# First folds by 128 columns, and the last left rows stored from GpSimd's queue

## Chip, cores, metric

One core of one Trainium2 chip. The metric is device time in microseconds of a whole launch; lower is better. Names in the profile: PE is the matmul engine (TensorE), DVE is VectorE, ACT is ScalarE; SyncE (SP) only issues DMAs (transfers between memories) and waits for them here.

## The reference, cut to what matters

```python
# four batches of N = 5824 rows, C = 256 channels
qn, kn = q / norm(q, axis=1), k / norm(k, axis=1)
a   = softmax(kn.T @ qn)                 # 256 x 256 per batch
x   = (v @ a).reshape(23296, 256)
out = ((x @ w1) * (x @ w2)) @ w3 @ w_out # d_ff = 1024
```

The kernel never forms `v @ a`. It *folds* the softmax matrix into the weights, `Wf = a @ [w1 | w2]` (256 x 2048 per batch), and multiplies v by that. Likewise `w3 @ w_out` is one matrix W. N is 45 x 128 + 64, so each batch ends in 64 "left" rows; the left rows of two batches are handled together.

## The kernel before, where the change and the argument touch it

Nearly all loads of q, k, v and the weights are issued by GpSimd; they cast f32 to bf16 on the way. An *eviction* below is the copy that takes a matmul's result out of its accumulation buffer. In batch 0 the softmax comes as soon as q and k are in, and the first folds stand between it and the first product tile:

```python
def quarter_mm(lo, c1, c2):                  # 256 columns of w1 and of w2
    ...
    for w in range(2):
        nc.tensor.matmul(m[:, w, :], lhsT=e[:, c2, c1 block], rhs=w12[:, c2, w, lo:lo+256], ...)
    if c2 == CT - 1:                         # evicted in two pieces of 128 columns
        for o in (0, P) if lo == 0 else ...:
            if c1 == 0: nc.scalar.activation(out=dst, in_=src, func=AF.Copy, scale=rs[:, c1])
            else:       nc.vector.tensor_scalar_mul(dst, src, rs[:, c1])

def first_folds():
    sum_mm(0)                                # row sums over the first half of the channels
    for c1 in range(CT): quarter_mm(0, c1, 0)
    sum_mm(1)                                # second half, then rs = 1 / sums
    for c1 in range(CT): quarter_mm(0, c1, 1)
```

The end of the kernel (`emit_out`, the small last chunk of a pair of batches; `B - 1` is the last batch):

```python
nc.vector.tensor_copy(o2, tl[1][:, 0, :])            # left rows of both batches
for m in (b - 1, b):
    k = (m - b + 1) * LEFT
    nc.sync.dma_start(out=out[m*N + NT*P : (m+1)*N, :], in_=o2[k : k + LEFT, :])
...
nc.scalar.copy(o[:, 0, :], tl[0][:, 0, :])
other = nc.scalar if b == B - 1 else nc.sync
other.dma_start(out=rows[:, NT - 1, :], in_=o[:, 0, :])
```

After this the framework adds, on each engine, a drain and a handshake that GpSimd collects. The drain is an instruction at the end of the engine's work: DVE's, for example, runs from 563.50 to 563.96 us, until just after DVE's last copy, which ends at 563.91.

## Time and profile before

| | before |
|---|---|
| time, median of 5 runs | 569.44 us (569.25 to 569.69) |
| span of the profiled execution | 567.7 us |
| PE busy | 557.6 us, 98% of the span, at a granted clock of 0.999 |
| chain that ended last | PE 93%, DMA 5%, ACT 1% |
| GpSimd's DMA instructions | 97, the last one at 492.32 us |

The prediction below takes the span apart, with the lines of the profile on which it rests.

### The profile page before, as it was taken

How to read it: one execution, taken by the hardware profiler on the slowest of the kernel's cores; microseconds unless marked ns; L12 is line 12 of the kernel's file. 1: busy time of each engine (PE TensorE's matmuls, PEld its weight loads, DVE VectorE, ACT ScalarE, POOL GpSimd, SP SyncE). 2: the span in 40 equal slices, each digit the busy share in tenths (PEclk: the TensorE clock that was granted, in tenths of full speed). 3: DMA queues.
4: the chain of work that ended last, by engine and by line, in shares of the span. 5: the costliest groups of instructions: out<-in, count | busy, mean ns of one | idle time of the engine just before them, and what ended most of it. 6: DMA issues, size and time to landing. Idle time of an engine off the chain costs nothing.

```text
span 567.7 us, 10095 instructions
## 1 busy us (share of the span) xinstructions
PE 557.6 (98%) x3755; PEld 355.4 (63%) x3755; DVE 375.4 (66%) x581; ACT 338.7 (60%) x627; POOL 77.9 (14%) x163
## 2 busy tenths in 40 slices
PE   8799999999999999999999999999999999999997
PEld 5664566776656666666656566666655655665655
DVE  1047645888966577888766668787876665565564
ACT  1057536777766577777675567777765554454453
POOL 4260013120111111121210101030120000000000
PEclk9999999999999999999999999999999999999999
DMA  9999989978455796595661595765740325221011
GB/s 213 211 182 209 173 171 237 226 164 192 115 142 121 143 192 148 90 193 123 145 149 75 97 219 117 155 120 121 185 112 39 85 74 149 64 68 71 38 70 61
DMA packets 75104, 77.45 MB, mean 136 GB/s; under 512 B 54192, under 2 KB 58800, under 8 KB 75056
## 3 DMA queue, kind: packets, MB, share of 16 engines
q0 software_dynamic: 15760, 38.93, 39.3%
q1 hardware_dynamic: 59008, 37.23, 22.0%
q10 hardware_dynamic: 288, 0.66, 0.4%
q8 instruction: 29, 0.48, 0.3%
q14 instruction: 19, 0.16, 0.1%
HBM read 78.91 MB, written 23.86 MB: 181 GB/s over the span
## 4 chain that ended last, share of the span: by engine, by line
PE 93%; DMA 5%; ACT 1%; POOL 0%; issue 0%; DVE 0%; ACTq 0%; POOLq 0%
PE o L521 28%; PE b L476 28%; PE a L476 28%; PE G L192 5%; DMA k<-in_k_dram 5%; PE fold L363 2%; PE w L649 1%; ACT kr L283 0%; PE quarter L389 0%; POOL k L111 0%; POOL q L111 0%; PE sqk L225 0%; PE row L271 0%; ACT e L322 0%; ACT Wf L398 0%
## 5 line engine op out<-in xcount | busy, mean ns | idle before, releaser
L497 DVE TENSOR_TENSOR abs<-as,b 128x512 bf16<-128x512 bf16 x336 | 230.6, 687 | 143.9 <-ACT as L482 131.4
L482 ACT CAST as<-a 128x512 bf16<-128x512 f32 (+1 forms) x384 | 215.9, 562 | 170.4 <-DVE abs L497 84.7
L476 PEld LDWEIGHTS <-Wf 128*128 128x128 bf16 x1536 | 149.0, 98 | 102.3 <-ACT Wf L398 0.6
L476 PE MATMUL a<-vT,Wf 128*128 128x512 bf16 x704 | 209.6, 379 | 0.4 <-ACT Wf L398 0.4
L476 PE MATMUL b<-vT,Wf 128*128 128x512 bf16 x704 | 209.6, 379 | 0.0
L521 PE MATMUL o<-W_sb,abs 128*128 128x256 bf16 x1344 | 201.5, 273 | 0.0
L521 PEld LDWEIGHTS <-abs 128*128 128x128 bf16 x1344 | 131.2, 98 | 79.8 <-issue 0.2
L201 DVE TENSOR_TENSOR acc<-acc,sq 128x1024 f32<-128x1024 f32 x66 | 80.4, 1219 | 0.6 <-ACT sq L189 0.6
L192 PE MATMUL G<-k,q 128*128 128x256 bf16 x276 | 49.8, 273 | 0.0
L189 ACT ACTIVATE sq<-q 128x512 f32<-128x512 bf16 x66 | 41.8, 633 | 0.0
L189 ACT ACTIVATE sq<-k 128x512 f32<-128x512 bf16 x66 | 41.5, 629 | 0.0
L464 POOL COPY gate_t<-abs 1x1 bf16<-1x1 bf16 x39 | 10.5, 269 | 171.7 <-DVE abs L497 168.8
L543 DVE COPY osb<-o 128x512 f32<-128x512 f32 x44 | 30.1, 685 | 0.9 <-PE o L521 0.9
L192 PEld LDWEIGHTS <-q 128*128 128x128 bf16 x276 | 27.0, 98 | 3.1
L542 ACT COPY osb<-o 128x512 f32<-128x512 f32 x44 | 25.8, 586 | 4.1 <-PE o L521 2.1
L468 POOL COPY gate_t<-vT 1x1 bf16<-1x1 bf16 x16 | 3.1, 193 | 158.8 <-DMA vT<-v 158.8
L111 POOL DMA_DIRECT2D q<-in_q_dram x28 | 15.1, 540 | 12.5 <-DMA k<-in_k_dram 5.5
L370 ACT ACTIVATE Wf<-fold,rs 128x512 bf16<-128x512 f32 x15 | 10.3, 687 | 10.9 <-PE fold L363 8.7
L283 ACT ACTIVATE kr<-row 128x256 f32<-128x256 f32 x1 | 0.4, 383 | 26.1 <-PE row L271 26.1
L363 PE MATMUL fold<-w,e 128*128 128x512 bf16 x56 | 15.0, 379 | 0.0
L487 DVE TENSOR_TENSOR left<-as,b 128x192 bf16<-128x192 bf16 x32 | 11.3, 354 | 5.1 <-ACT as L482 2.7
L497 DVE TENSOR_TENSOR abq<-as,b 128x512 bf16<-128x512 bf16 x16 | 10.8, 686 | 5.0 <-ACT as L482 4.5
(98 smaller groups left out, 242.3 us busy)
## 6 DMA issues: line engine op xcount, KB each, us to landing
out_dram<-osb SPq DMA_DIRECT2D x44, 512.0 KB, 3.3
k<-in_k_dram POOLq DMA_DIRECT2D x19, 512.0 KB, 8.3
v<-in_v_dram POOLq DMA_DIRECT2D x19, 512.0 KB, 5.2
q<-in_q_dram POOLq DMA_DIRECT2D x18, 512.0 KB, 5.8
w_wout<-in_moe_w_dram POOLq DMA_DIRECT2D x1, 2048.0 KB, 22.7
k<-in_k_dram POOLq DMA_DIRECT2D x4, 320.0 KB, 8.8
v<-in_v_dram POOLq DMA_DIRECT2D x4, 320.0 KB, 4.9
q<-in_q_dram POOLq DMA_DIRECT2D x3, 320.0 KB, 4.1
```

Of the source, the lines that this page charges most:

```text
L111: nc.gpsimd.dma_start(out=pieces[nm, n, pi][:, lo:hi, :], in_=qk_main[nm, n][0][:, pi * PIECE + lo : pi * PIECE + hi, :])
L189: nc.scalar.activation(out=dst[:, :, part, :], in_=src[:, o : o + 2, :], func=AF.Square)
L192: nc.tensor.matmul(G[:, ct, :], lhsT=qt[:, i, ct * P : (ct + 1) * P], rhs=kt[:, i, :], start=(pr == 0 and part == 0 and ct == 0), stop=(pr ...
L201: nc.vector.tensor_add(accs[n], accs[n], sqs[0])
L363: nc.tensor.matmul(m, lhsT=st["e"][:, c2, c1 * P : (c1 + 1) * P], rhs=w12[:, c2, w, lo:hi], start=(c2 == 0), stop=(c2 == CT - 1),)
L476: nc.tensor.matmul(t[:, :n], lhsT=Wf[b][:, ct, w, j * P : (j + 1) * P], rhs=rhs_of(b, c, ct), start=(ct == 0), stop=(ct == CT - 1),)
L482: nc.scalar.copy(a_sb[:, :n], tiles[0][:, :n])
L487: nc.vector.tensor_mul(both, a_sb[:, :n], tiles[1][:, :n])
L497: nc.vector.tensor_mul(ab, a_sb, tiles[1])
L521: nc.tensor.matmul(tl[h][:, o, :], lhsT=lhsT, rhs=W_sb[:, j, :], start=(j == 0 and o == 0), stop=(j == FT - 1 and (small or o == 1)), skip ...
L542: nc.scalar.copy(o[:, 0:2, :], tl[0])
L543: nc.vector.tensor_copy(o[:, 2:4, :], tl[1])
```

## The change

The intent: fold only the 128 columns that the first product tile needs, so that it starts sooner; and let the last two left stores leave side by side on two queues instead of one after the other on SyncE's.

```diff
-        def quarter_mm(lo, c1, c2):
+        def columns_mm(lo, width, c1, c2):
...
-                    m[:, w, :], lhsT=..., rhs=w12[:, c2, w, lo : lo + 256],
+                    m[:, w, :], lhsT=..., rhs=w12[:, c2, w, lo : lo + width],
...
         def first_folds():
             sum_mm(0)
             for c1 in range(CT):
-                quarter_mm(0, c1, 0)
+                columns_mm(0, P, c1, 0)
             sum_mm(1)
             for c1 in range(CT):
-                quarter_mm(0, c1, 1)
+                columns_mm(0, P, c1, 1)
+            for c1 in range(CT):
+                for c2 in range(CT):
+                    columns_mm(P, P, c1, c2)
...
-                        nc.sync.dma_start(out=out[m * N + NT * P : (m + 1) * N, :], in_=o2[k : k + LEFT, :])
+                        eng = nc.gpsimd if m == B - 1 else nc.sync
+                        eng.dma_start(out=out[m * N + NT * P : (m + 1) * N, :], in_=o2[k : k + LEFT, :])
```

More of the change, by code (lines that the diff above doesn't have):

```diff
@@ L378, in fold @@
                 fold_mm((w, c1, h * 512, (h + 1) * 512), c2, tag, i % 2 == 0 or (n == 0 and i == 7))
-        def quarter_mm(lo, c1, c2):
+        def columns_mm(lo, width, c1, c2):
             if c2 == 0:
-                tag = "ab" if lo == 0 else "out"
+                tag = "ab" if lo < 256 else "out"
                 st[lo, c1] = psum.tile(
-                    [P, 2, 256], F32, tag=tag, name=f"quarter_{lo}_{c1}", bufs={"ab": 4, "out": 3}[tag]
+                    [P, 2, width], F32, tag=tag, name=f"columns_{lo}_{c1}", bufs={"ab": 4, "out": 3}[tag]
                 )
@@ L389, in quarter_mm @@
                 nc.tensor.matmul(
-                    m[:, w, :], lhsT=st["e"][:, c2, c1 * P : (c1 + 1) * P], rhs=w12[:, c2, w, lo : lo + 256],
+                    m[:, w, :], lhsT=st["e"][:, c2, c1 * P : (c1 + 1) * P], rhs=w12[:, c2, w, lo : lo + width],
                     start=(c2 == 0 and w == 0), stop=(c2 == CT - 1 and w == 1), skip_group_check=True,
@@ L393, in quarter_mm @@
             if c2 == CT - 1:
-                for o in (0, P) if lo == 0 else (slice(0, 256),):
-                    cols = slice(o, o + P) if lo == 0 else o
-                    dst, src = Wf[n][:, c1, :, lo : lo + 256][:, :, cols], m[:, :, cols]
-                    if c1 == 0:
-                        nc.scalar.activation(out=dst, in_=src, func=AF.Copy, scale=st["rs"][:, c1 : c1 + 1])
-                    else:
-                        nc.vector.tensor_scalar_mul(dst, src, st["rs"][:, c1 : c1 + 1])
+                dst = Wf[n][:, c1, :, lo : lo + width]
+                if c1 == 0:
+                    nc.scalar.activation(out=dst, in_=m, func=AF.Copy, scale=st["rs"][:, c1 : c1 + 1])
+                else:
+                    nc.vector.tensor_scalar_mul(dst, m, st["rs"][:, c1 : c1 + 1])
         def first_folds():
@@ L412, in second_quarter @@
                 for c2 in range(CT):
-                    quarter_mm(256, c1, c2)
+                    columns_mm(256, 256, c1, c2)
         if n == 0:
```

## The prediction

> **What bounds the kernel now.** I read the page first: PE is busy 98% of a 567.7 us span at a granted clock of 0.999, and the chain that ended last is PE for 93% and DMA for 5%. The next question is where PE is *not* the bound. A table of stretches answers it:
>
> ```profile
> 30.45:37.27 6.82, 6.04 (x64) 4.56 (x64) 3.08 (x12) 3.46 (x10) 6.54 (x10) 1.00 1.17 157
> ...
> 563.66:567.68 4.02, 0.00 (x1) 0.00 (x0) 0.25 (x1) 0.37 (x1) 0.00 (x0) 0.81 0.24 65
> ```
>
> The columns are stretch and length, then busy time of PE, weight loads, DVE, ACT and POOL. The stretch between these two, 37.27 to 563.66, asked for by itself, has PE busy 526.36 of 526.39 us. So whatever moves the first product matmul at 37.27 moves all that follows, and only three pieces are not PE's: the input loads to 30.45 (untouched), the softmax and first folds to 37.27, and the tail of 4.02 us after the last matmul. The change touches the second and the third.
>
> The chain of waits in the second piece, in order of time (start, length, what):
>
> ```profile
> 35.18 0.52 ACT e L322
> 35.70 0.05 issue
> 35.75 0.20 PE sum L340 x2
> 35.95 0.46 PE quarter L389 x4
> 36.41 0.04 PE sum L340 x2
> 36.45 0.02 issue
> 36.47 0.18 DVE rs L348
> 36.65 0.02 issue
> 36.68 0.02 ACTq L398
> 36.69 0.04 issue
> 36.74 0.48 ACT Wf L398
> 37.22 0.05 issue
> 37.27 0.60 PE a L476 x2
> ```
>
> What to see: the four 256-column matmuls of the first half of the sum over channels (0.46 us) stand between the first and the second pair of row-sum matmuls; the row sums give the reciprocal, the reciprocal gives the eviction, and that gives the first product. Evictions are already 128 columns wide per w; the matmuls are not.
>
> The third piece, from the timeline and from the instructions of the kernel's end:
>
> ```profile
> 563.48 0.42 DVE L533 COPY oleft<-o 128x256 f32<-128x256 f32 x1 [0.55 <-PE o L521]
> ...
> 563.93 1.13 SPq L536 DMA_DIRECT2D out_dram<-oleft  x2
> 564.10 0.36 ACTq L540 DMA_DIRECT2D out_dram<-osb  x1
> ```
>
> ```profile
> L765 POOLq DRAIN x3: 46/102/8672, 492.2 to 567.4; - x3
> L765 SPq DRAIN x3: 7/7/13, 566.8 to 567.2; - x3
> L765 PEldq DRAIN x2: 13/369/725, 563.0 to 567.2; - x2
> ```
>
> SyncE issues the two left-row stores one after the other (starts 563.93 and 564.48). Its own waits in the trace pass at 566.25 (first left store, 2.31 after its start), 566.58 (ACT's 128 KB, 2.48 after 564.10) and 566.75 (second left store, 2.27). A closing handshake follows to 567.68; GpSimd collects it, and from its wait at 566.94 to the end are 0.74 us. The measured time is the span plus about 1.76 us (569.45 for the profiled execution).
>
> The second fence is the surprise. Its columns are count, min/median/max in ns, first and last start. Each engine ends with a drain. GpSimd's first one took **8672 ns**, and the order of records makes that one the start at 492.20, behind its last DMA instructions (491.80 and 492.32, the latter done generating at 492.88). It ended at 500.87, which is 8.0 us after the last descriptors and 4.4 us after that transfer landed (SyncE's wait for it passes at 496.43). GpSimd's other drains, with no DMA before them, took 102 and 46 ns. Today all this lies under 66 us of matmuls.
>
> **What the Trainium skill says.** (1) "TensorE: Matmul & The Clock Gate", section "Back-to-back issue gap": 134 cycles at 128 columns, 262 at 256, thus 56 and 109 ns at 2.4 GHz, though it gives 81 ns per matmul for a sustained stream with weight loads. The trace agrees with the first: the 128-column transposes start 55 ns apart, the 256-column folds 108. (2) "DMA: Bandwidth & Descriptors", section "Issuing engines are not separate DMA queues": queues share the same 16 engines and a second issuer saves only sequencer time. Here that is the 0.55 us between SyncE's two starts. (3) The same page, "Anatomy of one DMA — SWDGE (gpsimd) path": about 2.0 us fixed, mostly the receipt of the write. The 32 KB load that GpSimd issued at 491.80 landed in 1.9. (4) "VectorE: DVE Perf Modes", section "The DRAIN you can't avoid", says the drains at a kernel's ends are about 12 ns on all engines. SyncE's 7 and 13 ns agree; GpSimd's 8672 does not, and the measurement decides. No page that I found tells what that drain waits for.
>
> **Part one: the folds.** Nothing is removed in columns: eight 256-column matmuls become sixteen of 128. At 55 ns that is 16 x 0.055 = 0.88 us against 8 x 0.108 = 0.87. Evictions keep size and number (four of 473/466 ns on ACT and 484/474 on DVE). What moves:
> - The first four now take 4 x 0.055 = 0.22 and end their issue at about 36.03. The second exp ends at 36.09 and its weight load starts 0.05 later, at 36.14, already set by ACT. Only the row-sum matmul, now at 36.24, was held up by the fold in front, so it moves to about 36.15: **0.09 us**, not the 0.22 that the shorter folds suggest.
> - Reciprocal, ACT's semaphore and eviction follow: eviction 36.74 to about 36.65. Its own matmul ends issue near 36.27 plus 0.22 of latency = 36.49, no new bound. DVE's eviction of the other half, today 36.93 because its 256-column matmul ends late, moves to about 36.65 too; it needs 0.48 and ends at 37.13, beside ACT's.
> - The first product goes from 37.27 to about 37.18. The added second block of eight, 0.44 us from about 36.43, ends by 36.90, inside the hole in which PE waits for the eviction, so it costs nothing.
> - Buffers: the ring of four now has the four column tiles ahead of the first two product tiles. Those reuse exactly the tiles whose evictions they need anyhow.
> - Carried to the end? The nearest operand is the load that the transposes at 44.50 need: it lands at 34.76 + 9.6 = 44.36, 0.14 ahead, enough for 0.09.
>
> Part one: **-0.09 us**.
>
> **Part two: the store.** Removed from SyncE: one issue of 0.58 us. Added to GpSimd: one of about 0.53 us, after the same DVE copy (ends 563.91, or 563.82 shifted). From a GpSimd copy's end at 491.46 to the end of the following descriptors at 492.33 were 0.86 us, and the first packet came 0.70 later; elsewhere the first figure is as low as 0.67. So descriptors end near 564.6, packets start near 565.3 and, with the 1.16 us that SyncE's first left store took from first packet to landing, it lands near 566.4. ACT's store, unchanged at 566.58 - 0.09 = 566.49, would then land last. The gain is at most 566.75 - 566.58 = 0.17 us, not the 0.55 of the issue.
>
> Against it stands the drain, which now must follow this last store. If it takes 8.0 us after the last descriptors again: 564.6 + 8.0 = 572.6, + 0.74 = 573.3 span, + 1.76 = 575.1. If it takes 4.4 after landing instead: 566.4 + 4.4 = 570.8, + 0.74 + 1.76 = 573.3. I take the drain as real work that repeats, since it stands behind DMA instructions alone.
>
> **The rivals.**
> - *No drain of that length.* It may hang on the larger transfers before it (320 KB) or on something else that ended near 500.9 (SyncE's 0.52 us store issue ends then). For: one occurrence only, and a record of a sequencer instruction. Against: the two short drains had no DMA. Then 569.44 - 0.09 - (0 to 0.17) = 569.2 to 569.35. Chance 0.28.
> - *GpSimd's queue is slow to begin but the drain short*: a landing after 566.8 would give 569.4 to 569.8. The 1.9 us of the small load speaks against it. Within the same 0.28.
> - *The drain scales with outstanding bytes*: 64 KB instead of 352 KB would give something between, 570 to 573. Chance about 0.15. What is left, 0.57, is the two readings worked out above.
> - *Narrow matmuls at 81 ns* instead of 55: 16 x 0.081 = 1.3 us; the second block would end at 36.15 + 12 x 0.081 = 37.12, still inside the hole. The loss is nil, the gain stays.
>
> **Range and chances.** A small heap at about 569.3 (0.28), a thin stretch to 573 (0.15) and a large heap from 573 to 575.2 (0.57, the 8.0 reading more likely than the 4.4). The mixture has half its weight on each side at about 573.5 to 574; I give 574.0, which stands between the two drain readings. A range that holds 8 in 10 has to reach both heaps: 569.0 to 575.5. Two per cent are 11.4 us. The gains come to under 0.3 us and the worst drain reading costs 575.1 - 569.4 = 5.7, so "same" is nearly sure.
>
> **What would show it.** First product at 37.15 to 37.20, the second exp's row sum at about 36.15, PE without a hole from there to about 563.57. In the tail: one left store on SyncE's queue, one on GpSimd's, landings near 566.2 to 566.5, and a GpSimd drain of 6 to 9 us that begins near 564 and ends 0.7 us before the span does. If that drain lasts under 2 us, the central step is wrong and the time is about 569.3. If the first product has not moved, the reading that only the row-sum matmul was held is wrong.

## The result, and the profile after

The changed kernel takes 575.80 us (575.65 to 575.89, 5 runs) against 569.44: slower by 1.1%, or 6.4 us. The ratio is 1.0111, with a 95% interval of 1.0097 to 1.0125: a real loss, though "same" by a line drawn at 2%, as predicted. The measured time is above the predicted range (569.0 to 575.5).

The chain of waits of the changed kernel between the softmax and the first product (start, length, what):

```profile
35.73 0.20 PE sum L340 x2
35.93 0.24 PE columns L389 x4
36.18 0.15 PE sum L340 x2
36.33 0.26 PE columns L389 x4
...
36.63 0.48 ACT Wf L396
37.12 0.05 issue
37.16 0.60 PE a L477 x2
```

The four folds between the two row sums take 0.24 us instead of 0.46. The eviction starts at 36.63 instead of 36.74, the first product at 37.16 instead of 37.27. Yet the last matmul starts at 563.62, not 563.39. In the waits of the same kernel between 39 and 46 us (who waited for what: us in total, times, longest) is why:

```profile
PEld L363 <- DMA w<-in_moe_w_dram: 0.5, 1, 0.5
PEld L134 <- DMA v<-in_v_dram: 0.4, 1, 0.4
```

The weight loads of a fold and of a transpose now wait for loads from memory. The matmuls behind them start 0.16 and 0.14 us late (39.93 and 44.92). Those two loads took 0.5 us longer in this execution than in the profiled one of before (for instance 10.1 us instead of 9.6 for v's second piece).

The tail of the changed kernel, from the timeline, and its drains:

```profile
564.16 0.49 SPq L538 DMA_DIRECT2D out_dram<-oleft  x1
564.33 0.36 ACTq L542 DMA_DIRECT2D out_dram<-osb  x1
564.44 0.56 POOL L538 DMA_DIRECT2D out_dram<-oleft  x1 [71.33 <-DVE oleft L534]
```

```profile
L767 POOLq DRAIN  x3: 52/102/8659, 564.4 to 573.6; - x3
```

The last line is nearly the whole loss; the later last matmul adds 0.23 us to it. GpSimd's drain of 8659 ns existed before (8672 ns), but it began at 492.2, under the matmuls. Now it begins at 564.41, with the store, and ends at 573.07. SyncE had everything it waits for at 567.2, so the other engines stand still for nearly 6 us until GpSimd collects them. GpSimd's store landed at 567.04, long before the drain ended. ("The end of the descriptors" below is the end of GpSimd's own DMA instruction in the profile, here 564.99.)

### The profile page after: what moved, and what is told of

Read it like the earlier page. It is cut to its first block, busy times and chain, and to the rows that moved or that the text cites. A ratio compares the mean times of both kernels' runs of the same rounds, so it can differ in the third digit from the quotient of the medians.

```text
span 573.9 us, 10113 instructions
## 1 busy us (share of the span) xinstructions
PE 557.2 (97%) x3763; PEld 355.2 (62%) x3763; DVE 375.0 (65%) x581; ACT 338.7 (59%) x627; POOL 78.7 (14%) x164
## 4 chain that ended last, share of the span: by engine, by line
PE 79%; issue 13%; DMA 5%; ACT 1%; POOL 1%; DVE 0%; POOLq 0%; DVEq 0%
PE b L477 23%; PE o L522 23%; PE a L477 23%; PE G L192 5%; DMA k<-in_k_dram 5%; PE fold L363 2%; PE w L651 1%; DVE abs L498 0%; ACT kr L283 0%; PE columns L389 0%; POOL k L111 0%; ACT as L483 0%; POOL q L111 0%; PE sqk L225 0%; PE tr_I-625_626 L134 0%
```

## The experiments

Theory after this: the drain costs a fixed time once late work stands before it. Rivals: it scales with the bytes in flight; it is a delay after the last descriptors; it belongs to the library that GpSimd loads for its sums over partitions; and part one has a cost of its own.

### The two parts alone

**folds_only**: the changed kernel with `eng = nc.sync` for both left stores.

> Part one alone, both left stores on SyncE. Theory (all the loss is GpSimd's drain, and the 0.10 us that the first product gains is eaten by waits for loads): first product at 37.16 as in the changed kernel, last GpSimd drain hidden, 569.2 to 569.8 us, the same as before. Rival (the narrow folds cost something of their own later, as the last matmul 0.23 us later in the changed kernel's profile suggests): 569.7 to 570.0 in every round. A second rival (part one was a gain that the profile's late loads hid by chance): 569.3 or less in most runs.

569.40 us (569.24 to 570.03, 5 runs), before 569.55 (569.41 to 569.69), ratio 0.9999 (0.9985 to 1.0012). Part one neither costs nor gains anything that these runs resolve.

**store_only**: the kernel before with the store of the last left rows on GpSimd.

> Part two alone, old folds. Theory: the drain behind GpSimd's store carries it all, 575.5 to 575.9 us, as the changed kernel, with a drain of 8.6 to 8.7 us that begins within 0.6 us of the store. Rival (the two parts together do it): under 573.

575.34 us (575.27 to 576.48, 4 runs), ratio 1.0106 (1.0092 to 1.0120), closing drain 8659 ns. Part two carries the loss. The median lies 0.16 us under the range forecast, because PE was not late here: the profiled execution's last matmul starts at 563.28, against 563.62 in the changed kernel.

**store_act**: new folds, the last left store issued by ACT behind its own.

```diff
-                        eng = nc.gpsimd if m == B - 1 else nc.sync
-                        eng.dma_start(out=out[m * N + NT * P : ...], in_=o2[k : k + LEFT, :])
+                        if m < B - 1: nc.sync.dma_start(... as before ...)
                     other.dma_start(out=rows[:, NT - 1, :], in_=o[:, 0, :])
+                    if b == B - 1: nc.scalar.dma_start(out=out[b * N + NT * P : ...], in_=o2[LEFT:, :])
```

> New folds; the last left store goes behind ACT's own store on ACT's queue. Theory (a second HWDGE issuer, no GpSimd work at the end): 569.1 to 569.7, the end no earlier than before because ACT issues two one after the other. Rival (any store beside SyncE's two is late, whichever queue): over 570.

(HWDGE in the expectation: the queues of SyncE and ACT, which the profile lists as hardware_dynamic; GpSimd's is software_dynamic.) 569.48 us (569.42 to 570.16, 5 runs), ratio 1.0001 (0.9988 to 1.0013). It is GpSimd that is dear at the end, not a further issuer.

**folds_slack**: folds_only with the first fold of the upper half and two transposes moved later in PE's order (agenda times 1.7, 7.0 and 8.0 to 2.7, 9.0 and 10.0).

> New folds, stores as before, and the first fold of the upper half and two of the transposes moved later in PE's order, so that the loads they need (w1's upper half, v's second piece) have landed. Theory (loads landed 0.5 us later in that profile and took the gain): the two gaps of 0.16 and 0.14 us are gone, last matmul 0.1 us earlier than before's 563.39, 569.1 to 569.5. Rival (PE gives the gain back elsewhere, in evictions): gaps at other lines of the same sum, and 569.4 to 569.8.

569.36 us (569.31 to 570.13, 5 runs), ratio 1.0000 (0.9988 to 1.0013): inconclusive. In its profile the two waits are gone, but another stands there, in the list of waits between 62 and 68 us:

```profile
PE w L651 <- DMA w3T<-w_wout: 0.8, 1, 0.8
```

So the last matmul was later (564.08), not 0.1 us earlier: the expectation missed. Most runs of the kernels without a late drain, the one before included, lie at 569.2 to 569.8, others up to a microsecond higher (the kernel before reached 570.81). Two profiles of such higher runs, this one and drain_b2_copy below, each show PE idle for 0.8 us before one load. That spread is far larger than what part one can give.

### What the drain pays for

**late_copy**: no store from GpSimd, but one 1x1 copy behind DVE's last one.

```diff
+                    if b == B - 1:
+                        nc.gpsimd.tensor_copy(gate_t, o2[:1, :1])
```

> The kernel before with one 1x1 copy on GpSimd behind the last DVE copy, no DMA of GpSimd's after 493 us. Reading A (the drain is paid when any DMA went before it since the start, whenever that was): drain of about 8 us from 564.1, 574 to 575.5 us. Reading B (it counts from the last descriptors, something runs on for 8 us after them): a drain under 0.5 us, 569.3 to 569.8.

574.78 us (574.72 to 575.53, 4 runs), ratio 1.0089 (1.0074 to 1.0104). Its drain:

```profile
L767 POOLq DRAIN  x3: 46/93/8206, 564.0 to 572.7; - x3
```

This is reading A. The last DMA of GpSimd's was issued 71 us earlier and had long landed, and still the drain takes 8.2 us. It is not a delay that counts from the last descriptors, and here not a wait for a landing.

**store_16**: GpSimd stores 16 of the 64 rows, SyncE the other 48.

> Old folds; GpSimd stores only 16 of the last 64 left rows (16 KB), SyncE the other 48. If the drain is fixed: 575.4 to 575.9, drain 8.5 to 8.7. If it scales with bytes or rows: a quarter of it or some part, 570 to 573.

575.30 us (575.17 to 575.50, 4 runs; 0.1 under the forecast), drain 8621 ns: bytes and rows don't matter.

**store_both**: both left stores of the last pair on GpSimd (`if b == B - 1`).

> Old folds; GpSimd stores both left halves of the last pair, one after the other. If the drain counts 8.05 us from the last descriptors: the second set of descriptors ends 0.52 us later, so store_only plus 0.5, near 576.2. If it counts from the start of the drain's own record or from the first store: as store_only. If it adds for each DMA: 580 or more.

576.48 us (576.09 to 577.19, 4 runs), ratio 1.0116. The drain ends 8.15 us after the second set of descriptors; in store_only it ends 8.07 after the only one. (In the profiled execution PE was late as well: the last matmul starts at 564.10.)

**big_last**: GpSimd stores the last whole chunk (512 KB), the left rows stay with SyncE.

> Old folds; GpSimd stores the last whole chunk (512 KB), ready at 561.50, and SyncE both left stores as before. Fixed 8.05 us from the last descriptors (562.36, taking 0.86 from ready): drain ends near 570.4, plus 0.04, 0.75 and 1.76, so 573.0 us. From landing plus 4.4: landing near 565, 572. Scaling with bytes (eight times those of the left store): over 580.

573.10 us (573.05 to 573.27, 4 runs), ratio 1.0057. The drain (8637 ns) ends 8.07 us after the descriptors, as for 64 KB; eight times the bytes change nothing.

**big_prev**: the same for the chunk before it.

> Old folds; GpSimd stores the last chunk but one (512 KB), ready near 551.9, some 12 us before the left rows; all later stores as before. With a fixed 8.05 us from the last descriptors (about 552.8) the drain ends near 560.9, before the 566.9 at which GpSimd collects the others: 569.3 to 569.8, nothing lost. If any store of GpSimd's costs, wherever it stands: 571 or more.

569.58 us (569.37 to 569.80, 4 runs), ratio 0.9993. The drain is as long, but begins in time:

```profile
L766 POOLq DRAIN  x3: 52/93/8636, 551.9 to 567.3; - x3
```

Here a store from GpSimd is free, since the drain behind it ends at 560.56, before the others finish.

**no_library**: store_only without the loaded library: the sums over partitions and the call that loads their code become plain copies (wrong result).

> store_only without the loaded library: the three sums over partitions and the call that loads their code are replaced by plain copies. The result is wrong on purpose. If the 8 us belong to the loaded library (a switch back at the end): closing drain under 1 us, about 569.5. If they belong to the DMA path or to every late drain: closing drain 8.6 us, 575 to 576.

575.43 us (one run, state unknown), wrong result as meant, drain 8650 ns. It is not the library.

**mid_drain_copy** and **mid_drain_store**: late_copy and store_only with one line more, before the last matmuls are emitted, where GpSimd has just issued its last load:

```diff
+    nc.gpsimd.drain()
     n = len(pend)
```

> late_copy plus an explicit drain on GpSimd behind its last load, at about 493 us, where it is hidden. Reading A1 (a drain pays for DMAs that no drain has yet followed): the explicit drain takes about 8 us, the closing drain behind the copy under 0.5 us, 569.3 to 569.8 us. Reading A2 (the closing drain takes 8 us behind any late work of GpSimd's, whatever was drained): 574.7 to 575.6 as late_copy.

> store_only plus the same explicit drain at about 493 us. If the drain's length grows with the number of DMAs since the last drain (some 80 in the kernel, one here): the closing drain is far shorter, under 2 us, and the time 569.5 to 570.5. If one DMA is enough for the full length: 575.2 to 575.9, closing drain 8.6 us.

569.43 us (569.23 to 569.51, 4 runs; ratio 0.9990, 0.9975 to 1.0005) and 569.68 us (569.65 to 569.95, 4 runs; ratio 0.9996, 0.9980 to 1.0013). The drains of the two kernels' ends, the copy's first:

```profile
L768 POOLq DRAIN  x3: 34/93/267, 563.8 to 567.2; - x3
```

```profile
L767 POOLq DRAIN  x3: 46/93/2701, 564.2 to 567.6; - x3
```

The explicit drains took 8672 and 8676 ns at 492 us, hidden, and the closing ones only 267 ns and 2701 ns. So the 8 us are paid for DMAs that no drain has yet followed. mid_drain_store's drain missed its forecast of under 2 us: the 2701 ns ended at 566.88, with the landing of GpSimd's store (SyncE's wait for it passed at 566.82). The drain waits for a landing too, but that is the smaller part.

**drain_b1_copy**, **drain_b2_copy**, **drain_b3_copy**: is it a lump sum, or so much for each DMA? late_copy with the explicit drain at the start of batch 1, 2 or 3:

```diff
     for b in range(B):
+        if b == 1:            # 2, 3
+            nc.gpsimd.drain()
         make_agenda(b)
```

> late_copy with the explicit drain at about 171 us, some 44 of the 97 GpSimd DMAs (37% of the packets) behind it. Grows with the number: closing drain about 3.6 us (3.0 if with the packets), explicit one about 4.4. Fixed sum, paid once: closing drain 0.27, explicit one 8.0. Full whenever more than a few DMAs lie behind: both 8.

> The same with the explicit drain at about 291 us, some 22 DMAs (19% of the packets) behind it. Number: closing drain about 1.9 us (1.6 by packets). Fixed sum, once: 0.27. Full for more than a few: 8.

> The same with the explicit drain at about 417 us, 4 DMAs (3% of the packets) behind it. Number or packets: 0.4 to 0.6 us. Fixed sum, once: 0.27. Full for any: 8.

All three are correct, at 570.53, 570.36 and 569.57 us (one run each, state unknown). Their closing drains, in this order:

```profile
L769 POOLq DRAIN  x3: 46/102/3867, 564.1 to 568.5; - x3
```

```profile
L769 POOLq DRAIN  x3: 46/102/2154, 564.9 to 568.3; - x3
```

```profile
L769 POOLq DRAIN  x3: 51/102/591, 564.1 to 567.5; - x3
```

| DMA instructions of GpSimd's since its last drain (counted in the trace) | closing drain behind the copy, ns | less 267, per DMA |
|---|---|---|
| 0 (mid_drain_copy) | 267 | |
| 4 (drain_b3_copy) | 591 | 324 / 4 = 81 |
| 23 (drain_b2_copy; 22 expected) | 2154 | 1887 / 23 = 82 |
| 44 (drain_b1_copy) | 3867 | 3600 / 44 = 82 |
| 97 (late_copy) | 8206 | 7939 / 97 = 82 |

A straight line: **82 ns for each DMA instruction** that GpSimd issued since its last drain. Packets don't fit: of 15760 packets on this queue, 37% lie behind the drain at 171 us, which would give 2.9 us over the 267 ns, where 3.6 was measured. Nor does GpSimd's other work: its other operations since the last drain (5, 22, 41 and 66 copies, sums and the like, counted in the same traces) would cost 65 to 120 ns each. What the drain does in these 82 ns, no run shows.

The explicit drains of these three kernels, in the same order, don't follow the line so simply. For the first about 4.4 us were forecast, and 9.4 measured:

```profile
L720 POOLq DRAIN  x1: 9389/9389/9389, 171.0 to 171.0; - x1
```

```profile
L720 POOLq DRAIN  x1: 10936/10936/10936, 291.0 to 291.0; - x1
```

```profile
L720 POOLq DRAIN  x1: 10974/10974/10974, 413.5 to 413.5; - x1
```

The third stood behind a sum over partitions that ended at 416.80; from there to its end are 7.69 us, and 93 DMAs x 82 ns are 7.6. The first two do not fit: from the last descriptors to their ends are 8.74 and 10.26 us, where 53 and 74 DMAs would give 4.3 and 6.1. In both a load of k was still on its way (landed at 178.14 and 298.88), and from that landing to the drain's end are 2.21 and 3.07 us, half of 4.3 and 6.1 and a little more. So it looks as if half of the sum is paid before the wait for the last landing and half after it. That also fits the drain at 492 us in the kernel before, which shows no extra time: half of its 97 DMAs' sum, counted from 492.88, ends at 496.9, after the last landing at 496.42. No run tested this; the 82 ns hold where no load lands later than that half.

**after_mid_drain**: the changed kernel with that one line at 493 us.

> The changed kernel with the explicit drain at about 493 us. Theory: the closing drain ends with the landing of GpSimd's store, near 566.9, so 569.3 to 569.8 us, the whole loss gone and no gain left, since that landing is no earlier than the 566.75 of SyncE's second store before. If the change had a gain of its own of 0.17 or more in the tail, 569.2 or less.

569.61 us (569.42 to 569.82, 5 runs), before 569.44 (569.25 to 570.68, 9 runs), ratio 0.9996 (0.9983 to 1.0010). The loss is gone and no gain is left over. No version that I ran beats the kernel before beyond the scatter.

## Why the prediction was right or wrong

**Right: what decides.** The step "the drain now must follow this last store" and "real work that repeats" held: it was the drain of full length, not a late queue and not narrow matmuls. What sets its length was not known, and the reading that came true did so by luck (see the drain's cause).

**Wrong: the number and the range.** The reading that came true was the 8.0 us one, worked out as 575.1. The number given, 574.0, was a mixture with the readings "4.4 after landing", "scales with bytes" and "no drain of that length", of which store_16, big_last and late_copy leave none. And the range ended at 575.5 although the 8.0 reading itself was mis-sized by half a microsecond. The failed step of that sum is its first term above all, "after the same DVE copy (ends 563.91, or 563.82 shifted)": the copy ended at 564.14 (all terms from the profiled execution, 575.65 us):

| term | predicted | measured | difference |
|---|---|---|---|
| DVE's last copy ends | 563.82 | 564.14 | +0.32 |
| from there to the end of GpSimd's descriptors | 0.78 | 564.99 - 564.14 = 0.86 | +0.08 |
| from there to the end of the drain | 8.0 | 573.07 - 564.99 = 8.07 | +0.07 |
| from there to the end of the span | 0.74 | 573.86 - 573.07 = 0.79 | +0.05 |

The sum is 0.52, and 575.1 + 0.52 = 575.6. I had a measured 0.86 for the second term in front of me and took less. The other 0.15 us up to the median is the scatter of the runs.

**The largest term, 0.32, is part one's.** The mechanism was right and exact: from the landing of the last k load (start plus length in the chain of waits) to the first product are 6.82 us in the kernel before and in store_only and late_copy 6.82 and 6.81, and 6.72 in the changed kernel and in folds_only, 6.73 in store_act and after_mid_drain. That is the predicted 0.09. The step that failed under it is "enough for 0.09", and with it "PE without a hole from there": the slack of 0.14 before the load of v was taken from one execution, and loads moved by 0.5 us between executions. The load that the fold at 39.93 waits for, which the prediction did not look at, was late as well (landed 39.89, against 39.39 in the profile before). From the first product to the start of the last matmul pass 526.12 or 526.13 us where no load is late (before, store_only and late_copy with old folds; store_act and after_mid_drain with new ones), 526.46 in the changed kernel's profile and 526.41 in folds_only's. Old folds are not safe from it: store_16 shows 526.33, drain_b3_copy 526.36. So part one's 0.09 us exists, survived in two of the five profiles with new folds, and cannot be seen in medians.

**The drain's cause.** "8.0 us after the last descriptors" fitted by luck, because this kernel has one such drain and 97 or 98 DMAs before it: 98 x 0.082 = 8.04 against the 8.07 measured. The reading as a delay behind the last DMA is refuted by late_copy; the sum for each DMA is shown by the five drains of the table, none of which had a transfer of GpSimd's still on its way.

**The gain of part two.** "Lands near 566.4" was off: GpSimd's store landed at 567.04 in the changed kernel (2.60 us after its start) and at about 566.82 in mid_drain_store, where PE was not late. SyncE's second store had landed at 566.75. So the 0.17 us were never there, with or without the drain.

## What to carry to other kernels

Before moving the last work of a kernel to an engine that has been idle, look at what that engine does at the close: a long wait at the end of an engine's stream is invisible until something late is put in front of it. For GpSimd's queue, count the DMAs it issued; behind any late instruction of its own, even a copy, the closing drain costs 82 ns for each of them here, unless an explicit drain in an idle stretch has paid before (one issued while loads are on their way held GpSimd for 10.9 us here). A gain of a tenth of a microsecond at the head of a stream is worth nothing while loads behind it scatter by half a microsecond.

## What the Trainium skill lacked or had wrong

- "VectorE: DVE Perf Modes", section "The DRAIN you can't avoid", tells of two kinds: one behind every VectorE operation, and the runtime's own, about 12 ns on all engines. The drains of this document carry a line of the kernel, and it is not shown that they are of either kind. SyncE's are 7 and 13 ns, the longest of PE, DVE and ACT 725, 464 and 370, and GpSimd's is 267 ns behind a copy plus 82 ns for each DMA since its last drain, 8206 ns for 97. I found no page that gives a drain such a cost for each DMA.
- "DMA: Bandwidth & Descriptors" compares the queues by their first byte but not by what they cost at the close. Here the kernel with one 64 KB store from GpSimd took 575.34 us, against 569.55 for the kernel before; with one explicit drain 72 us earlier it took 569.68.
- The same page's section "Issuing engines are not separate DMA queues" holds: with the drain out of the way, the second issuer gained nothing measurable (ratio 0.9996).
